# Attention and a mixture of experts on one core: one pass over all tokens per expert, with operands made ahead

## The chip, the core and the metric

The kernel runs on one core of a Trainium2 chip. The engines of a core work side by side, each with its own queue, in order: TensorE (PE in the profile, its weight loads PEld) multiplies matrices, VectorE (DVE) and ScalarE (ACT) do elementwise work and read TensorE's results from PSUM banks, GpSimd (POOL) does little here, and SyncE (SP) issues the transfers between DRAM and the on-chip memory (SBUF). The metric is the time of one execution on the device in microseconds (us), the median over runs.

## The reference

```python
scores = scale * q @ k.T + bias(relative position)      # B, H, S, D = 4, 8, 576, 64
attn = softmax(scores); x = (attn @ v), tokens 2304 x 512
P = exp(x @ w_gate - max); 8 times: rows, then columns normalised    # 2304 x 8
out = sum over e of P[:, e] * (relu(x @ w1[e]) @ w2[e])  # w1: 8 x 512 x 1024, w2: 8 x 1024 x 512
```

The inputs are float32 and are drawn at random.

## The kernel before, in words

The first 550 us or so are attention, with expert 0 of the mixture woven into its second half. The change doesn't touch that part. What follows is the mixture for experts 1 to 7, and everything here is about it.

Each float32 operand is held as two float16 parts, high and low, and a product is three matmuls (high with high, high with low, low with high). The tokens lie in four blocks of 512 and one of 256 (blocks 0 to 3, and 4). For experts 1 to 7 both layers are done with the Strassen-Winograd scheme: seven products of half-size operands in place of eight. The seven left operands of layer 1 are A11, A12, S2, S3, S1, A22, S4, made of the quarters of w1; the seven of w2 are B11, T4, B21, T2, T3, T1, B22. They sit in 14 slots (6 tiles `slot`, and 8 places in `area` where expert 0's weights were). On the token side four sums T1 to T4 per block are needed (`xt`, made by `t_prep`), beside the tokens themselves (`xa`, `xb`, `xc`).

- `l1(i)` (L1453) does layer 1 of a block: `prod1` (L1468) issues the matmuls of one product, ScalarE takes the banks out (`snap`, L1539), VectorE forms sums, and `put` (L1527 on ScalarE, L1179 or L1533 on VectorE) cuts them into high and low parts in the tiles `h`.
- `l2(i)` does layer 2 (`prod2`, L1502), with `out_` (L1591) and the addition into the accumulators `acc`, one tile of 512 columns per 128 tokens.
- `w_load` fetches the four quarters of a weight into `raw` (those of w2 lie in `xc`, over tokens), `w_max` (L1375) finds the largest magnitude on ScalarE, and `bcast_nodes` (L1205, L1210) spreads it over the partitions with two small matmuls.
- `w_make(e, w)` then makes the seven operands of a weight: sums of quarters on VectorE (L1422) and cuts into high and low (L1412 on ScalarE, L1179 on VectorE, both of 1024 columns). It writes them straight into slots, and stores a copy to DRAM (`sc_w`).

The tokens are passed over in two runs. The first takes blocks 0, 4 and 1 through experts 1 to 7, and makes the operands of the next expert at the last block of the present one, since a slot is free only when its last product is done. The second takes blocks 2 and 3 through experts 7, 1, ..., 6, and gets the operands back from DRAM (`w_fetch`). All accumulators of a run (10 tiles) stay on the chip.

The order of the instructions isn't the program's: `Plan` (a list scheduler) records each piece of work with its engine, an assumed duration, the names that it reads and writes, and a priority, and writes out each engine's queue in the order of its own assumed start times. Transfers are assumed to take 0.1 us on SP and to land 4 us later (5 us for a fetch). On the chip every queue then runs in that order, and an instruction that waits holds up those behind it. The last lines are the two runs:

```python
    runs = [
        (list(range(1, E)), [(0, pairs(0, 0)), (2, pairs(2, 4)), (1, pairs(1, 1))]),
        ([E - 1] + list(range(1, E - 1)), [(0, pairs(0, 2)), (1, pairs(1, 3))]),
    ]
...
                if last and nxt:
                    ready(nxt, 0)
                l2(i, bt, f"pcol{e}", pcols[e], n == len(experts) - 1)
                if last and nxt:
                    ready(nxt, 1)
```

## Time and profile before

| what | value |
|---|---|
| median of 3 runs | 1891.71 us (1890.39 to 1895.35) |
| the profiled execution | 1893.5 us, its span 1891.7 us |
| PE busy | 1688.3 us, 89% of the span |
| DVE busy | 1472.5 us, 78% |
| ACT busy | 1109.2 us, 59% |
| mean granted clock of TensorE | 0.952 of full speed |
| moved by DMA | 259.24 MB |

The profile comes from one execution; its span runs from the first to the last instruction, and the execution's own time is 1.8 us longer. "Busy" is the time in which an engine has an instruction in work. A granted clock of 1.00 is 2.4 GHz, 0.50 is 1.2 GHz; a number between is a mean over a stretch with both. In a time order "[4.82 <-ACT ...]" behind a row says that the engine stood for 4.82 us before it, and what released it.

### The profile page before, as it was taken

The page shows a single profiled execution, that of the slowest core. Times are in us where ns is not written, and L with a number is a line of the kernel's source. Part 1 is how long each engine was busy: PE and PEld are TensorE (multiplying, and loading weights), DVE is VectorE, ACT ScalarE, POOL GpSimd, SP SyncE. Part 2 cuts the span into 40 slices and gives each one's busy share as a digit, 9 for nine tenths or more (in the row PEclk, how much of TensorE's full clock was granted, in tenths as well). Part 3 has the DMA queues.
Part 4 walks back from the last instruction along what each step waited for, and adds up shares of the span by engine and source line. Part 5 has one row for each costly group of instructions (what it writes and reads, how often), then busy time and mean ns, then how long its engine had stood idle before and what let it go on. Part 6 is the DMA issues. An engine that isn't in the chain of part 4 may idle for free.

```text
span 1891.7 us, 39544 instructions
## 1 busy us (share of the span) xinstructions
PE 1688.3 (89%) x16286; PEld 1362.6 (72%) x16286; DVE 1472.5 (78%) x2767; ACT 1109.2 (59%) x2050; POOL 1.5 (0%) x10
## 2 busy tenths in 40 slices
PE   7676587887889599898989999898999999999998
PEld 4344354554556388787868888787888888888887
DVE  8898877877868878888887979888767666766765
ACT  7686877877866645665655646554444334434433
POOL 0000000000000000000000000000000000000000
PEclk9898699899999899998989999899999999999999
DMA  8989999999986502405042323301314314314221
GB/s 289 252 191 229 208 193 215 211 215 202 228 206 219 204 1 86 161 34 212 24 146 79 145 102 136 111 1 60 98 42 150 124 34 157 103 55 157 80 83 40
DMA packets 316149, 259.24 MB, mean 137 GB/s; under 512 B 225856, under 2 KB 269632, under 8 KB 315328
## 3 DMA queue, kind: packets, MB, share of 16 engines
q1 hardware_dynamic: 315968, 256.72, 49.2%
q8 instruction: 127, 2.08, 0.4%
q14 instruction: 54, 0.44, 0.1%
HBM read 141.19 MB, written 62.39 MB: 108 GB/s over the span
## 4 chain that ended last, share of the span: by engine, by line
PE 65%; DVE 13%; DMA 11%; ACT 6%; issue 3%; SPq 1%; DVEq 0%; ACTq 0%
PE bankA L1482 16%; PE bankA L1502 12%; PE bankB L1502 9%; PE bankE L1502 8%; PE bankE L1482 7%; DMA aT<-ah 7%; PE bankB L1482 4%; PE l L202 3%; PE pv L202 2%; PE s L202 2%; ACT area L202 2%; DVE area L202 2%; DVE ah L202 1%; DMA xc<-in_moe_w_dram 1%; DVE sb L202 1%
## 5 line engine op out<-in xcount | busy, mean ns | idle before, releaser
L1482 PEld LDWEIGHTS <-slot 128*128 128x128 f16 x5040 | 453.2, 98 | 67.8 <-issue 20.9
L1502 PEld LDWEIGHTS <-hA 128*128 128x128 f16 x2268 | 223.4, 99 | 28.9 <-DVE hA L1179 0.8
L202 PEld LDWEIGHTS <-area 128*128 128x128 f16 x2465 | 152.2, 100 | 120.3 <-issue 52.6
L1502 PEld LDWEIGHTS <-area 128*128 128x128 f16 x1512 | 150.6, 101 | 63.7 <-ACT area L1527 25.5
L1482 PE MATMUL bankE<-xt,slot 128*128 128x256 f16 (+1 forms) x1680 | 186.3, 263 | 7.8 <-ACT p L1539 6.1
L1482 PE MATMUL bankA<-xt,slot 128*128 128x256 f16 (+1 forms) x1680 | 184.9, 262 | 4.8 <-ACT u L1539 3.2
L1527 ACT ACTIVATE hA<-c 128x512 f16<-128x512 f32 x189 | 118.1, 627 | 117.8 <-DVE c L1179 117.0
L1502 PEld LDWEIGHTS <-hS 128*128 128x128 f16 x1512 | 147.5, 98 | 18.7 <-issue 1.5
L202 DVE SCALAR_TENSOR_TENSOR ah<-sb,st,ah 128x576 f16<-128x576 f32 x144 | 114.1, 814 | 37.6 <-ACT ah L202 37.0
L1585 ACT COPY u<-bankA 128x512 f32<-128x512 f32 (+1 forms) x70 | 37.9, 542 | 174.1 <-PE bankA L1502 174.0
L1179 DVE SCALAR_TENSOR_TENSOR hA<-c,hA 128x512 f16<-128x512 f32 x189 | 128.1, 686 | 13.9 <-ACT hA L1527 11.3
L202 ACT ACTIVATE ah<-sb,st 128x576 f16<-128x576 f32 x144 | 106.6, 770 | 49.7 <-DMA aT<-ah 40.4
L1502 PE MATMUL bankB<-area 128*128 128x256 f16 x756 | 101.9, 292 | 36.4 <-ACT area L1527 24.1
L202 PE MATMUL s<-qkT 128*128 128x512 f16 (+3 forms) x560 | 87.8, 310 | 51.7 <-DVE st L202 47.5
L202 ACT ACTIVATE sb<-sb,st,sms 128x576 f32<-128x576 f32 x144 | 123.5, 859 | 0.7
L202 PE MATMUL l<-area 128*128 128x512 f16 x413 | 110.2, 382 | 7.3 <-ACT ys L202 2.6
L1179 DVE SCALAR_TENSOR_TENSOR acc<-c,fs,acc 128x256 f32<-128x256 f32 x252 | 110.2, 481 | 2.2
L202 PEld LDWEIGHTS <-qkT 128*128 128x128 f16 (+1 forms) x560 | 39.2, 105 | 92.6 <-issue 68.5
L202 PE MATMUL pv<-aT,vs 128*64 128x256 f16 (+3 forms) x1176 | 80.0, 269 | 27.3 <-DMA aT<-ah 25.7
L1539 ACT ACTIVATE u<-bankA 128x512 f32<-128x512 f32 x126 | 75.0, 595 | 38.9 <-PE bankA L1482 24.6
L202 PEld LDWEIGHTS <-vs 128*64 128x64 f16 (+1 forms) x1176 | 54.4, 116 | 55.8 <-issue 49.9
L1539 ACT ACTIVATE p<-bankA 128x512 f32<-128x512 f32 x63 | 37.6, 597 | 96.2 <-PE bankA L1482 65.1
(210 smaller groups left out, 3213.9 us busy)
## 6 DMA issues: line engine op xcount, KB each, us to landing
sc_w<-area SPq DMA_DIRECT2D x48, 512.0 KB, 3.6
area<-sc_w SPq DMA_DIRECT2D x48, 512.0 KB, 4.3
bt<-sc_bias SPq DMA_DIRECT2D x32, 576.0 KB, 4.8
sc_w<-slot SPq DMA_DIRECT2D x36, 512.0 KB, 2.7
slot<-sc_w SPq DMA_DIRECT2D x36, 512.0 KB, 4.6
raw<-in_moe_w_dram SPq DMA_DIRECT2D x28, 512.0 KB, 5.1
xc<-in_moe_w_dram SPq DMA_DIRECT2D x28, 512.0 KB, 5.7
area<-const_xm_dram SPq DMA_DIRECT2D x40, 128.0 KB, 3.8
```

What stands on the lines that cost most here:

```text
L202: self.plan.record(self.name, cost, lambda: fn(*args, **kw), ins, outs, move)
L1179: vec.scalar_tensor_tensor(out=o, in0=x, scalar=s, in1=y, op0=op0, op1=op1)
L1482: pe.matmul(ps[:, jf * w : jf * w + w], t[:, a, c * 512 + f * P : c * 512 + f * P + P], x(xp, c), start=(first and jf == 0 and c == 0 and ...
L1502: pe.matmul(ps[:, j * 256 : j * 256 + 256], h[:, a, fc * w + j * P : fc * w + j * P + P], t[:, wp, fc * 256 : fc * 256 + 256], start=(firs ...
L1527: on_act(0.58, lambda: act.activation(h[:, 0, sl], x, AF.Relu if relu else AF.Copy), [r], wk)
L1539: on_act(0.55, lambda: act.activation(tmp[k], bank[b], f, scale=HS), [b], [k], 0)
L1585: on_act(0.27 * nt, lambda: act.copy(tmp[k][:, :n], bank[b][:, :n]), [b], [k], 0)
```

## The change

There is one pass. For each expert all five blocks are visited, in the order here, 0, a, 4, b, where the next expert starts with b: its token sums and accumulators are kept on the chip. For other blocks the sums `xt` (now two buffers) come from DRAM (`sc_t`), the accumulators (now 8 tiles, two sets of 4) are written to and read from `sc_y`, and one of blocks 1 to 3 at a time lies in `xc`. Blocks 1 and 2 give their places (`xb` and half of `xc`) to the raw quarters of w2. The sums of three of the five blocks are made during expert 1 rather than before it.

The operands of experts 2 to 7 are made in single steps (`w_steps`): a cut into one of two staging tiles, and at most one sum of quarters. One step is let go at each call of `paced()`, which stands after each half of a block's layer 1 and twice in layer 2; a step's ScalarE part can't be planned before the product that was last at that call (`mark`). The cut is stored to DRAM, and all 14 operands are fetched into the slots at the change of expert. The core of the diff:

```diff
-    raw.append({q: xc[:, i // 2].bitcast(F32)[:, 1024 * (i % 2) : 1024 * (i % 2) + 1024] for i, q in enumerate(BLK)})
+    raw.append(
+        {q: (xb, xc[:, 0])[i // 2].bitcast(F32)[:, 1024 * (i % 2) : 1024 * (i % 2) + 1024] for i, q in enumerate(BLK)}
+    )
     slot = [fin.tile([P, 2, 1024], F16, name=f"slot{i}") for i in range(6)]
     slot += [w1t[0][i] for i in range(4)] + [w2t[0][i] for i in range(4)]
-    XK = [["x0"], ["x1"], ["raw111", "raw112"], ["raw121", "raw122"], ["x4"]]
+    XK = [["x0"], ["raw111", "raw112"], ["raw121", "raw122"], ["x3"], ["x4"]]
     XALL = [k for l in XK for k in l]
-    acc = [fin.tile([P, DM], F32, name=f"acc{t}") for t in range(10)]
+    acc = [fin.tile([P, DM], F32, name=f"acc{t}") for t in range(8)]
...
+    mark = [0]
+    def on_unit(cost, fn, r, w):
+        mark[0] += 1
+        on_pe(cost, fn, r, [*w, f"mark{mark[0]}"])
...
-    xt = [fin.tile([P, 4, 2, 2, w], F16, name=f"xt{i}") for i, w in enumerate((256, 256, 128))]
-    sc_x = dram.tile([2, P, 2, 4096], F16, name="sc_x")
+    xt = [fin.tile([P, 4 * 2 * 2 * 256], F16, name=f"xt{i}") for i in range(2)]
+    sc_x = dram.tile([3, P, 4096], F16, name="sc_x")
+    sc_t = dram.tile([5, P, 4096], F16, name="sc_t")
     sc_w = dram.tile([E - 2, 2, 7, P, 2048], F16, name="sc_w")
+    stage = [fin.tile([P, 2, 1024], F16, name=f"stage{i}") for i in range(2)]
+    for i in range(4):
+        tmp[f"g{i}"] = stage[i // 2][:, i % 2].bitcast(F32)
...
-            i = old[USE[w][len(new)]] if old else 7 * w + len(new)
-            new[op] = i
-            t, r = slot[i], raw[w][q]
-            rk = f"raw{w}{q}"
-            on_act(1.04, lambda: act.activation(t[:, 0], r, AF.Copy, scale=s), [rk, f"scal{e}{w}"], [f"w{i}"], 2)
-            on_vec(1.27, lambda: stt(t[:, 1], r, s, t[:, 0], ALU.mult, ALU.subtract), [rk, f"scal{e}{w}"], [f"w{i}"], 2)
-            if e < E - 1:
-                k = USE[w].index(op)
-                dma(sc_w[e - 1, w, k], t.rearrange("p a n -> p (a n)"), [f"w{i}"], [f"sw{e}{w}{k}"])
+            k, r = USE[w].index(op), raw[w][q]
+            rd, at = [f"raw{w}{q}", f"scal{e}{w}"], [f"mark{mark[0]}"]
+            if e == 1:
+                t, tk, at = slot[7 * w + k], [f"w{7 * w + k}"], []
+            else:
+                j = turn[0] % 2
+                t, tk = stage[j], [f"g{2 * j}", f"g{2 * j + 1}"]
+                turn[0] += 1
+            on_act(1.04, lambda: act.activation(t[:, 0], r, AF.Copy, scale=s), rd + at, tk, 2)
+            on_vec(1.27, lambda: stt(t[:, 1], r, s, t[:, 0], ALU.mult, ALU.subtract), rd, tk, 2)
+            if e > 1:
+                dma(sc_w[e - 2, w, k], t.rearrange("p a n -> p (a n)"), tk, [f"sw{e}{w}{k}"])
...
+            plan_ = (
+                ("A11", "11"),
+                ("A22", "22", ("22", "21", "22", ALU.add)),
+                ("A12", "12", ("21", "11", "21", ALU.subtract)),
+                ("S3", "21", ("11", "22", "11", ALU.subtract)),
+                ("S2", "11", ("12", "12", "11", ALU.subtract)),
+                ("S1", "22"),
+                ("S4", "12"),
+            )
         else:
...
+        def step(op, q, *sums):
+            put(op, q)
+            for a in sums:
+                tt(*a)
+        return [lambda a=a: step(*a) for a in plan_]
...
+    seq, here = [], 3
+    for e in range(1, E):
+        a, b = (x for x in (1, 2, 3) if x != here)
+        seq += [(e, x) for x in ((here, 0, a, 4, b) if e < E - 1 else (here, 0, a, b, 4))]
+        here = b
+    visits, visit = [], []
+    for n, (e, b) in enumerate(seq):
+        if n == 0 or seq[n - 1][1] != b:
+            visits.append((e, b))
+        visit.append(len(visits) - 1)
+    todo = []
+    def paced():
+        if todo:
+            todo.pop(0)()
...
+    def t_make(b, z, ts, src):
+        x = xts(b, z)
+        t_prep(xv[src], XK[src], WID[b], [x[:, k] for k in range(4)], [[f"t{z}{k}"] for k in range(4)], ts)
+        n = 16 * WID[b]
+        dma(sc_t[b, :, :n], xt[z][:, :n], [f"t{z}{k}" for k in range(4)], [f"st{b}"])
+    def t_ready(r):
+        if r >= len(visits):
+            return
+        (e, b), z = visits[r], r % 2
+        if e == 1:
+            t_make(b, z, ("g0", "g1", "g2", "g3"), at(b))
+            return
+        m = 16 * WID[b]
+        dma(xt[z][:, :m], sc_t[b, :, :m], [f"st{b}"], [f"t{z}{k}" for k in range(4)])
+    def x_ready(n):
+        if seq[n][1] in (0, 4):
+            return
+        for _, b in seq[n + 1 :]:
+            if b not in (0, 4):
+                if b != seq[n][1]:
+                    dma(xc[:, 1], sc_x[b - 1], [f"sx{b}"], XK[3])
+                return
+    def acc_ready(r):
+        if r >= len(visits):
+            return
+        (e, b), z = visits[r], r % 2
+        if e == 1:
+            first_part(tiles_of(b, z))
+            return
+        for t, a in tiles_of(b, z):
+            dma(acc[a], sc_y[t], [f"y{t}"], [f"acc{a}0", f"acc{a}1"])
+    def acc_done(r, e):
+        b, z = visits[r][1], r % 2
+        if e < E - 1:
+            for t, a in tiles_of(b, z):
+                dma(sc_y[t], acc[a], [f"acc{a}0", f"acc{a}1"], [f"y{t}"])
...
+    w_load(2, 0)
+    w_max(2, 0)
+    acc_ready(0)
+    acc_ready(1)
+    for n, (e, b) in enumerate(seq):
+        r = visit[n]
+        i, at_end, leaves = (b, r % 2), n % 5 == 4, visit[n + 1 : n + 2] != [r]
+        nxt = e + 1 if e < E - 1 else None
+        if n % 5 == 0:
+            gate_col(e)
+            if nxt:
+                w_load(nxt, 1)
+                w_max(nxt, 1)
+                todo.extend(w_steps(nxt, 0) + w_steps(nxt, 1))
+                if nxt < E - 1:
+                    todo.insert(7, lambda e=nxt + 1: (w_load(e, 0), w_max(e, 0)))
+        l1(i)
+        x_ready(n)
+        if leaves:
+            t_ready(r + 2)
+        if at_end and nxt:
+            assert len(todo) <= 7
+            w_fetch(nxt, 0)
+        l2(i, pairs(b, r % 2), f"pcol{e}", pcols[e], e == E - 1)
+        if leaves:
+            acc_done(r, e)
+            acc_ready(r + 2)
+        if at_end and nxt:
+            assert not todo, len(todo)
+            w_fetch(nxt, 1)
```

Three places where the order of the instructions moves. The first is VectorE before the change, where layer 1 of expert 2's first block meets the end of w2's operands (`xc` holds raw quarters of w2, `area` the slots; `c`, `s` and `h` belong to layer 1, `acc` to layer 2):

```order
L1422 TENSOR_TENSOR xc_73<-xc_73 128x1024
L1533 TENSOR_TENSOR area_100<-c211_6686,area_100 128x512
L1422 TENSOR_TENSOR xc_73<-xc_73 128x1024
L1179 SCALAR_TENSOR_TENSOR area_100<-xc_73,fs15_6735,area_100 128x1024 x2
L1422 TENSOR_TENSOR xc_73<-xc_73 128x1024
L1179 SCALAR_TENSOR_TENSOR area_100<-xc_73,fs15_6735,area_100 128x1024
L1591 TENSOR_TENSOR c110_6681<-bankB0_6669,p1_6675 128x512
L1179 SCALAR_TENSOR_TENSOR area_100<-xc_73,fs15_6735,area_100 128x1024
L1179 SCALAR_TENSOR_TENSOR acc0_6697<-c110_6681,fs41_6762,acc0_6697 128x256
L1179 SCALAR_TENSOR_TENSOR acc1_6698<-c110_6681,fs41_6762,acc1_6698 128x256
L1179 SCALAR_TENSOR_TENSOR area_100<-xc_73,fs15_6735,area_100 128x1024
```

And VectorE after the change, in the middle of expert 4, whose blocks go on while expert 5's operands of w2 are made (`xb` and `xc` hold the raw quarters, `stage` the staging tiles):

```order
L1179 SCALAR_TENSOR_TENSOR c211_6686<-c211_6686,s2_6680 128x512
L1555 TENSOR_TENSOR hS3_6709<-c111_6682,hS3_6709 128x512
L1438 TENSOR_TENSOR xb_72<-xb_72 128x1024
L1555 TENSOR_TENSOR area_100<-c211_6686,area_100 128x512
L1614 TENSOR_TENSOR c110_6681<-bankB0_6669,p1_6675 128x512
L1179 SCALAR_TENSOR_TENSOR stage0_6726<-xc_73,fs27_6747,stage0_6726 128x1024
L1179 SCALAR_TENSOR_TENSOR acc0_6697<-c110_6681,fs43_6764,acc0_6697 128x256
L1179 SCALAR_TENSOR_TENSOR acc1_6698<-c110_6681,fs43_6764,acc1_6698 128x256
L1438 TENSOR_TENSOR xb_72<-xc_73,xb_72 128x1024
```

Eight operations of 1024 columns stood close together; now they stand one or two at a time between the operations of a block.

The second place is SP before the change, at a change of expert in the first pass: stores of the finished operands and loads of the next raw quarters.

```order
L1176 DMA sc_w_6727<-slot1_6692 128x2048
L1176 DMA raw21_6689<-in_moe_w1_dram 128x2x512
L1176 DMA sc_w_6727<-slot2_6693 128x2048
L1176 DMA raw22_6690<-in_moe_w1_dram 128x2x512
L1176 DMA raw11_6687<-in_moe_w1_dram 128x2x512
L1176 DMA sc_w_6727<-area_100 128x2048 x2
L1176 DMA raw12_6688<-in_moe_w1_dram 128x2x512
L1176 DMA sc_w_6727<-area_100 128x2048 x3
L1176 DMA xc_73<-in_moe_w2_dram 128x4x256
L1176 DMA sc_w_6727<-area_100 128x2048
L1176 DMA xc_73<-in_moe_w2_dram 128x4x256
```

SP after the change, at the change from the second to the third expert: the last accumulators of block 4 leave and those of another block come in, then the operands are fetched.

```order
L1176 DMA acc5_6702<-sc_y_70 128x512
L1176 DMA acc4_6701<-sc_y_70 128x512
L1176 DMA slot0_6691<-sc_w_6725 128x2048
L1176 DMA slot1_6692<-sc_w_6725 128x2048
L1176 DMA slot2_6693<-sc_w_6725 128x2048
L1176 DMA slot3_6694<-sc_w_6725 128x2048
L1176 DMA slot4_6695<-sc_w_6725 128x2048
L1176 DMA slot5_6696<-sc_w_6725 128x2048
L1176 DMA area_100<-sc_w_6725 128x2048 x3
L1176 DMA sc_w_6725<-stage1_6727 128x2048
L1176 DMA xc_73<-in_moe_w2_dram 128x4x256
L1176 DMA area_100<-sc_w_6725 128x2048 x5
```

The slots are now filled from `sc_w` at each change of expert; no store or load of the kept block's accumulators stands around the fetches. One staging store is still queued among the fetches.

The third place is SP after the change, at the change from the first to the second expert:

```order
L1176 DMA sc_w_6725<-stage0_6726 128x2048
L1176 DMA slot2_6693<-sc_w_6725 128x2048
L1176 DMA sc_w_6725<-stage1_6727 128x2048
L1176 DMA slot4_6695<-sc_w_6725 128x2048
L1176 DMA slot5_6696<-sc_w_6725 128x2048
L1176 DMA area_100<-sc_w_6725 128x2048 x2
L1176 DMA xc_73<-in_moe_w2_dram 128x4x256
L1176 DMA area_100<-sc_w_6725 128x2048
L1176 DMA sc_w_6725<-stage1_6727 128x2048
L1176 DMA xb_72<-in_moe_w2_dram 128x4x256
L1176 DMA area_100<-sc_w_6725 128x2048
```

Here three staging stores stand among the fetches.

## Rows read from the trace of the kernel before

**Rows 1.** Busy time of each engine by stretch, in us from the span's start: the start up to TensorE's first full expert, one row per expert in the first pass, one for the first expert of the second pass and one for the rest up to TensorE's end. Columns: stretch, length, busy time (instructions) of PE, PEld, DVE, ACT, POOL, granted clock, DMA share, GB/s.

```profile
630.05:744.03 113.98, 94.11 (x909) 82.99 (x908) 88.09 (x149) 67.34 (x107) 0.00 (x0) 0.91 0.20 71
744.03:848.30 104.27, 96.44 (x933) 84.88 (x931) 88.22 (x143) 61.37 (x97) 0.00 (x0) 0.97 0.31 112
...
952.70:1058.70 106.00, 97.22 (x933) 85.10 (x931) 88.28 (x143) 61.13 (x97) 0.00 (x0) 0.95 0.31 110
1058.70:1162.00 103.30, 95.99 (x933) 84.60 (x931) 88.30 (x142) 61.06 (x97) 0.00 (x0) 0.97 0.31 113
...
1370.56:1443.99 73.43, 73.43 (x674) 65.75 (x672) 49.24 (x83) 32.82 (x56) 0.00 (x0) 1.00 0.35 113
1443.99:1884.20 440.21, 440.21 (x4034) 394.42 (x4031) 295.50 (x493) 185.35 (x312) 0.00 (x0) 1.00 0.28 90
```

**Rows 2.** The order of time on TensorE: products at the start, two of the small block (24 matmuls of 128 columns), the pair of small matmuls that spreads a maximum, two successive wide products of the second pass, and the last one. Columns: start, length of the merged row, engine, line, operation, operands, shape, count.

```profile
630.05 2.88 PE L1482 MATMUL bankA<-xa,slot 128*128 128x256 f16 x24
...
666.42 0.27 PE L1205 MATMUL bankS<-ident,fs 128*1 128x128 f32 x1
...
685.92 0.38 PE L1210 MATMUL bankS<-fs,ones 1*128 1x1 f32 x2
...
694.16 1.50 PE L1482 MATMUL bankB<-xa,slot 128*128 128x128 f16 x24
695.50 1.50 PE L1482 MATMUL bankA<-xt,slot 128*128 128x128 f16 x24
...
1370.56 1.47 PE L1482 MATMUL bankA<-xa,slot 128*128 128x256 f16 x12
1371.87 1.47 PE L1482 MATMUL bankE<-xt,slot 128*128 128x256 f16 x12
...
1881.54 2.78 PE L1502 MATMUL bankB<-area 128*128 128x256 f16 x24
```

**Rows 3.** The order of time on all engines at the change from expert 1 to expert 2.

```profile
775.19 1.22 DVE L1422 TENSOR_TENSOR xc<-xc 128x1024 f32<-128x1024 f32 x1
775.39 0.60 PE L1502 MATMUL bankB<-area 128*128 128x256 f16 x2 [4.82 <-ACT area L1527]
...
778.06 2.48 DVE L1179 SCALAR_TENSOR_TENSOR area<-xc,fs,area 128x1024 f16<-128x1024 f32 x2
...
780.45 3.09 PE L1502 MATMUL bankB<-area,hA 128*128 128x256 f16 x24
```

**Rows 4.** Groups of instructions of VectorE from 675 us to the end: the cuts (L1179 on 1024 columns) and the sums (L1422) of the weights of experts 2 to 7. Columns: line, engine, operation, out<-in, shapes, count | busy us, mean ns | idle before.

```profile
L1179 DVE SCALAR_TENSOR_TENSOR area<-xc,fs,area 128x1024 f16<-128x1024 f32 x42 | 53.1, 1279 | 0.0
L1179 DVE SCALAR_TENSOR_TENSOR slot<-raw,fs,slot 128x1024 f16<-128x1024 f32 x36 | 46.0, 1279 | 0.0
...
L1422 DVE TENSOR_TENSOR xc<-xc 128x1024 f32<-128x1024 f32 x24 | 29.3, 1220 | 0.0
L1422 DVE TENSOR_TENSOR raw<-raw,raw 128x1024 f32<-128x1024 f32 x24 | 29.3, 1219 | 0.0
...
L1179 DVE SCALAR_TENSOR_TENSOR area<-raw,fs,area 128x1024 f16<-128x1024 f32 x6 | 7.7, 1281 | 0.0
```

**Rows 5.** Two stretches of 25 us, one of the first pass and one of the second, in the columns of rows 1.

```profile
825.00:850.00 25.00, 25.00 (x232) 22.40 (x230) 23.27 (x35) 17.43 (x25) 0.00 (x0) 1.00 0.14 56
...
1425.00:1450.00 25.00, 25.00 (x232) 22.41 (x229) 16.10 (x29) 8.77 (x15) 0.00 (x0) 1.00 0.66 220
```

**Rows 6.** The transfers: the first row is SP's own time for the issue of one (ns, least, median and most); in the others count, KB each and the median us from issue to landing.

```profile
L1176 SPq DMA_DIRECT2D sc_w<-slot x36: 319/320/382, 593.9 to 1170.4; - x36
...
sc_w<-area SPq DMA_DIRECT2D x48, 512.0 KB, 3.6
area<-sc_w SPq DMA_DIRECT2D x48, 512.0 KB, 4.3
...
sc_w<-slot SPq DMA_DIRECT2D x36, 512.0 KB, 2.7
slot<-sc_w SPq DMA_DIRECT2D x36, 512.0 KB, 4.6
...
acc<-sc_y SPq DMA_DIRECT2D x18, 256.0 KB, 3.0
...
sc_y<-s SPq DMA_DIRECT2D x6, 256.0 KB, 4.4
```

**Rows 7.** Who waited for whom: ScalarE for raw weights (800 to 1890 us), and SP for sums that were being stored (614 us to the end). Columns: total us, times, longest us.

```profile
ACT junk L1375 <- DMA xc<-in_moe_w_dram: 10.5, 10, 1.6
...
SPq L1176 <- DMA sc_y<-s: 7.9, 2, 5.2
```

**Rows 8.** The order of time at the start of the MoE part (token sums, L1330; the first stops of TensorE; ScalarE's wait for raw weights) and at the end (the last additions).

```profile
570.14 1.29 DVE L1330 TENSOR_TENSOR xt<-c,xt 128x512 f16<-128x512 f32 x2
...
653.89 0.37 PE L1205 MATMUL bankS<-ident,fs 128*1 128x128 f32 x1 [14.00 <-DVE fs L1384]
...
657.71 1.06 ACT L1375 ACTIVATE junk<-xc 128x1024 bf16<-128x1024 f32 x1 [1.52 <-DMA xc<-in_moe_w_dram]
...
659.39 2.72 PE L1482 MATMUL bankE<-xt,slot 128*128 128x256 f16 x12 [5.12 <-ACT p L1539]
...
1884.66 0.69 DVE L1591 TENSOR_TENSOR c<-bankB,u 128x512 f32<-128x512 f32 x1
1885.38 0.88 DVE L1179 SCALAR_TENSOR_TENSOR acc<-c,fs,acc 128x256 f32<-128x256 f32 x2
```

More of the change, by code (lines that the diff above doesn't have):

```diff
@@ L1613, in l2 @@
         out_(bb, "p1", c1, 0, 0)
+        if nt == 2:
+            paced()
         prod2(i, "S2", "T2", ba, False)
@@ L1664, in first_part @@
             )
-    def pairs(i, b):
-        if i == 2:
-            return [((16, 8), (17, 9))]
-        return [((4 * b + j, 4 * i + j), (4 * b + 2 + j, 4 * i + 2 + j)) for j in range(2)]
-    runs = [
-        (list(range(1, E)), [(0, pairs(0, 0)), (2, pairs(2, 4)), (1, pairs(1, 1))]),
-        ([E - 1] + list(range(1, E - 1)), [(0, pairs(0, 2)), (1, pairs(1, 3))]),
-    ]
-    TS = (("c110", "c220", "c210", "u4"), ("c111", "c221", "c211", "p7"))
-    def t_here(i):
-        dk = [[f"t{i}{k}"] for k in range(4)]
-        t_prep(xv[place[i]], XK[place[i]], WID[i], [xt[i][:, k] for k in range(4)], dk, TS[i % 2])
@@ new lines, in attention_sinkhorn_moe, with pairs, tiles_of @@
+    visits, visit = [], []
[7 more added lines that the diff above has]
+            todo.pop(0)()
+    def pairs(b, z):
+        if b == 4:
+            return [((16, 4 * z), (17, 4 * z + 1))]
+        return [((4 * b + j, 4 * z + j), (4 * b + 2 + j, 4 * z + 2 + j)) for j in range(2)]
+    def tiles_of(b, z):
+        return [ta for pair in pairs(b, z) for ta in pair]
```

119 lines of the change are left out of this document (37 added, 82 removed).

## The prediction, made before the result was known

> **What bounds the kernel now.** I read the stretches of the run first, one per expert, then the time order at the places where TensorE stands still, then the groups of VectorE, then the transfers.
>
> The stretches [rows 1] cut the MoE part where TensorE starts an expert's first block. In the second pass over tokens (from 1370.56 us) TensorE is busy for the whole of 73.43 us and of 440.21 us, at granted clock 1.00. There an expert's two blocks of 512 tokens take 73.43 us, so one block takes 36.7. In the first pass an expert's three blocks take 103.3 to 106.0 us, TensorE is busy for 96 to 97 of them, and the granted clock is 0.95 to 0.98. What would they take without standing still? Two blocks are 73.4. The small block has 7 products of 24 narrow matmuls, whose starts lie 1.34 us apart, and 7 of 12 wide ones at 1.31 [rows 2]: 18.55. That is 92.0 us.
>
> Now the whole. TensorE takes up the Strassen products at 630.05 and starts its last 24 matmuls at 1881.54 [rows 2]; these take 2.62, so it ends at 1884.16: 1254.1 us. Seven experts over four large blocks and one small need 7 x (4 x 36.71 + 18.55) = 1157.8. Two products (2.6) ran before 630.05, and twelve pairs of tiny matmuls that spread a weight's maximum cost 0.27 + 0.38 each [rows 2], 7.8. So 1163.0 is work and 91.1 is lost:
> - 630.05 to 744.03, the start: 114.0 less 92.0 - 2.6 + 1.3 = 90.7 leaves 23.3 lost.
> - 744.03 to 1370.56, six changes of expert: 626.5 less 6 x 92.0 and ten pairs (6.5) leaves 68.0, or 11.3 a change.
> - after that: nothing.
>
> Why is a change lost? At 775 us TensorE has stood for 4.82 us for an operand that ScalarE has only just written, and VectorE, with no gap, is in the middle of the next expert's weights (L1422, L1179 on 1024 columns); the matmuls after it run at 3.09 us per 24 where 2.62 is usual [rows 3], at a lower granted clock [rows 1]. The weights of six experts are 84 cuts and 48 sums, 165.4 us of VectorE [rows 4], 27.6 per expert. They can be written only when the old operands have been read for the last time, so all 27.6 fall between the last block's first layer and the next expert's second layer. The blocks ask VectorE for 49.24 us per two [rows 1], 24.6 each. So 24.6 + 27.6 = 52.2 us of VectorE meet about one block of TensorE, 36.7: 15.5 too much, of which 11.3 show.
>
> **The change part by part.** *Making operands at a pace.* Nothing is removed from VectorE: the same 84 cuts and 48 sums. They go to a staging tile, from there to DRAM, and are fetched into the slots at the change of expert, as the second pass does today. Per expert VectorE then has four large blocks (98.5), a small one (the first pass's 88.3 less 49.2 and 27.6, so 11.5) and the making (27.6): 137.6 of 165.4 us, 83%. Does TensorE keep going at that? Between 825 and 850 us VectorE is busy 23.27 of 25 (93%), with weights in it, and TensorE 25.00 [rows 5]. I therefore take the 68.0 as gone. Bounds: 0 to 68.0 kept.
>
> *Fetches at the change.* Fourteen of 512 KB, landing 4.6 and 4.3 us after their issue [rows 6], each released by the slot's last product and wanted one layer of a block (18.3 us) later. In the second pass the same 14 come and TensorE does not wait. New beside them: the last few staging stores and the next raw weights, some 5.7 MB in 18.3 us (seven fetches 3.7, two stores and two quarters 2.0), about 310 GB/s; the busiest stretch of the second pass has 220 GB/s at a DMA share of 0.66 [rows 5], so 310 would be a share of 0.93. Over a whole expert 28 operand transfers and 8 quarters of 0.52 MB, 14 accumulator tiles of 0.26 each way, and 5.5 MB of sums and tokens make 32 MB in 165.4 us, 190 GB/s. Cost 0; if a fetch lands 15 us late, that cover is gone.
>
> *Sums and accumulators that move.* Of 35 block visits 6 follow the same block and keep all. At the other changes accumulators go out and come in: 84 stores and 84 loads more of 256 KB, 22 more of sums, 12 more of tokens. From VectorE's last addition that is four issues (0.3 each), a landing (4.4, sc_y), four issues, a landing (3.0) [rows 6]: about 10 us. The two buffers are wanted again after one whole other visit, 18.6 us at the least. Cost by that: 0. Each change adds a wait at SP: the load stands until its store has landed, and behind it stand staging stores, raw loads and token loads. Who waits for those? A staging tile is reused two cuts later, and ScalarE, which writes it first, has TensorE's evacuations queued behind. No row shows this wait; the nearest are ScalarE's waits for raw weights, at most 1.6 us, 10.5 in 10 [rows 7]. So between 0 and 24 x 1.6 = 38 us; a gain has no way in. Most are covered, as those ten are: I take 5.
>
> The Trainium skill (DMA: Bandwidth & Descriptors, section "Two DMAs through the same engine are not ordered") says that a transfer which reads what an earlier one wrote must be held by its issuer until the earlier one has completed. The trace agrees: SP stood 7.9 us in two such waits for sc_y [rows 7]. By the rule alone SP stands 24 x 4.4 = 106 us more, out of 1160: that speaks against the change, and it is the rival "queue" below.
>
> The same page (section "Latency and other measured facts") gives 0.2 us as an average HBM access and 2 us under high load. By that a staging store would land up to 1.8 us later in the fuller traffic, and 84 of them would hold ScalarE by up to 151 us in all. The trace shows 2.7 and 3.6 us for the two kinds of store [rows 6], both among raw loads; I go by those.
>
> *The start.* Before 660 us TensorE waits 14.00 us and 5.12 us; VectorE runs without a gap through weights and token sums, then ScalarE waits for raw weights [rows 8]. The change takes three of five token-sum preparations out of here: 24 instructions of 512 columns, of which two take 1.29 (a second one adds 0.60), and 12 of half the width, taken at half of that: 18.0 us of VectorE. Bounds: 0 to 18.0 gained. The 14.00 us ended with VectorE, so a shorter list cuts them; the waits for raw weights stay. I take 13.3, so 10 of the 23.3 remain.
>
> *The first expert.* The same 18.0 us come back there: 137.6 + 18.0 = 156 of 165.4, 94%, just above the stretch that ran full. Its last staging stores also stand among its fetches. Bounds 0 to 18.0; I take 5.
>
> *The end.* The last block is the small one: the last two additions (0.69 and 0.88 us [rows 8]) at most halve: under 0.8 us, left out.
>
> Sum: 1893.5 (the profiled execution; span 1891.7) - 91.1 = 1802.4 with nothing lost, + 10 + 5 + 5 = **1822 us**. The median of the runs is 1891.71, 1.8 below the profiled one; less than I can resolve.
>
> **Rivals.**
> - *The bunch stays in part.* The last steps of each set still meet the change, because a step is released only after a marked product and its store must land before the fetch. For: in the order, stores stand among the first expert's fetches. Against: from the second expert on only one does. Half of 68.0 kept: 1822 + 34 = 1856.
> - *The start gains nothing* and the first expert pays for the moved sums: 1802.4 + 23.3 + 18.0 + 5 = 1849. For: the start also waits for the maxima of the second expert's weights, which remain. Against: VectorE's list there is 18.0 us shorter.
> - *Queue (slower than before).* Every change of block holds SP, and with it a staging store, ScalarE and TensorE. It turns the sign once a change costs more than (1893.5 - 1822) / 24 = 3.0 us; a whole landing of 4.4 beside what I took gives 1822 + 106 = 1928. For: each load does wait at SP for its store, as those two did [rows 7]. Against: SP's issues last 0.32 us [rows 6], and TensorE never waited at the second pass's fetches.
> - *The change does not do what it says.* Excluded for the kept blocks: the order shows no accumulator transfer at the expert changes.
>
> **How the numbers follow.** My forecast (1804 to 1836) 0.66; the bunch in part 0.16 and the start 0.08 (together 1836 to 1860, with tails above); queue 0.07, of which 0.05 is slower; everything hidden, below 1804, 0.03. The range 1802 to 1855 leaves out some 0.17. A change below 0.3% (5.7 us) can't be told from none: faster 0.92, same 0.03, slower 0.05.
>
> **What would show it.** Right: TensorE full across each change of expert, a period of about 165 us per expert at clock 1.00; VectorE near 83%; the idle time before the first 24-matmul product of expert 2 down to some 15 us; the DMA rate near 190 GB/s throughout. Wrong: TensorE waiting for a slot's fetch at the changes; ScalarE waiting for staging stores on sc_w; VectorE waiting for token loads in the first expert; or 30 us and more of TensorE idle between 640 and 800.

## The result, and the profile after

The changed kernel takes 1838.25 us (median of 4 runs, 1835.5 to 1842.19) against 1893.53 us before (4 runs, 1890.39 to 1895.92): a ratio of 0.9711, 95% interval 0.9686 to 0.9736. The profiled execution took 1839.06 us. The forecast was 1822 (1802 to 1855). Of the 71.5 us that it expected to go from the profiled 1893.5, 54.4 went. What it got right, and where the other 17 us stayed, is read from the stretches first. As in [rows 1] they are cut per expert: an expert's layers are 4 x 336 + 252 = 1596 matmuls, and each stretch begins with the first of the next 1596, because TensorE now begins an expert's first products before the last ones of the expert before. Columns as in [rows 1].

```profile
613.14:819.09 205.95, 185.15 (x1663) 158.14 (x1661) 174.23 (x307) 121.44 (x201) 0.00 (x0) 0.96 0.45 153
819.09:993.64 174.55, 168.89 (x1605) 150.45 (x1603) 139.72 (x228) 93.46 (x155) 0.00 (x0) 0.99 0.58 205
993.64:1161.79 168.15, 166.96 (x1605) 149.42 (x1602) 135.72 (x223) 91.52 (x150) 0.00 (x0) 1.00 0.53 190
1161.79:1328.78 166.99, 166.47 (x1605) 149.69 (x1602) 137.92 (x225) 90.32 (x148) 0.00 (x0) 1.00 0.55 193
...
1664.44:1831.61 167.17, 165.78 (x1598) 148.84 (x1595) 112.10 (x189) 69.95 (x119) 0.00 (x0) 1.00 0.25 75
```

An expert's matmuls need 4 x 36.71 + 18.55 = 165.4 us, and a stretch also holds up to two pairs of small matmuls that spread a maximum, 0.65 us each [rows 2] (the counts include instructions that reach over a border). Experts 3 to 7 together take 1831.61 - 993.64 = 838.0, of which 827 are these matmuls and 4.6 are seven such pairs: some 6 us lost in five experts. Expert 2 loses 174.55 - 165.4 - 1.3 = 8. In expert 1's stretch 64 other instructions begin, above all 48 matmuls of expert 0 at 0.22 us, together some 13.6 us; 205.95 - 165.4 - 13.6 leaves 27 lost. So 35 of the 41 us that these stretches lose lie in the first two experts.

A change of expert was where [rows 3] had TensorE standing. These 25 us, in the same columns, hold the changes from expert 2 to 3 (993.64) and from 3 to 4 (1161.79):

```profile
980.00:1005.00 25.00, 25.00 (x230) 22.23 (x228) 14.74 (x31) 7.97 (x14) 0.00 (x0) 1.00 0.52 188
1150.00:1175.00 25.00, 25.00 (x230) 22.23 (x228) 17.18 (x37) 10.16 (x18) 0.00 (x0) 1.00 0.50 169
```

TensorE is full, at granted clock 1.00, and VectorE has room (it is busy for 14.7 and 17.2 of 25 us). The making of weights still costs VectorE what it did [rows 4]: a cut takes 1279 ns, a sum 1218.

```profile
L1179 DVE SCALAR_TENSOR_TENSOR stage<-raw,fs,stage 128x1024 f16<-128x1024 f32 x35 | 44.6, 1279 | 0.5 <-ACT stage L1429 0.5
...
L1438 DVE TENSOR_TENSOR raw<-raw,raw 128x1024 f32<-128x1024 f32 x20 | 24.4, 1218 | 0.0
```

The transfers (count, KB, median us from issue to landing), beside [rows 6]:

```profile
sc_w<-stage SPq DMA_DIRECT2D x84, 512.0 KB, 3.2
acc<-sc_y SPq DMA_DIRECT2D x102, 256.0 KB, 3.8
area<-sc_w SPq DMA_DIRECT2D x48, 512.0 KB, 4.8
sc_y<-acc SPq DMA_DIRECT2D x84, 256.0 KB, 2.3
...
slot<-sc_w SPq DMA_DIRECT2D x36, 512.0 KB, 5.3
```

Fetches land 0.5 to 0.8 us later than before. Stores do not: a staging store takes 3.2, between the 2.7 and 3.6 of the two old kinds. The waits that the forecast could only bound are there now (600 to 1840 us; columns as in [rows 7]):

```profile
ACT stage L1429 <- DMA sc_w<-stage: 18.4, 10, 2.9
...
SPq L1176 <- DMA sc_y<-acc: 21.9, 25, 3.6
...
SPq L1176 <- DMA sc_w<-stage: 16.0, 7, 4.3
```

SP stood 21.9 us in 25 waits for a leaving accumulator, where the rule quoted ahead of the result gave 106 at 4.4 each: 0.9 us a wait, not a whole landing.

Now the first expert, where the loss is. The order of time on TensorE shows its two longest stops:

```profile
654.75 5.06 PE L1524 MATMUL bankB<-area,hA 128*128 128x256 f16 x23 [4.96 <-DVE area L1179]
...
783.22 0.37 PE L1504 MATMUL bankE<-xt,slot 128*128 128x256 f16 x1 [7.81 <-ACT xt L1340]
784.31 5.07 PE L1504 MATMUL bankE<-xt,slot 128*128 128x256 f16 x23 [0.71 <-DVE xt L1342]
```

The first is what is left of the start [rows 8]: 4.96 us for the last operands of w2, where before there were 14.00 and 5.12. In the first and the last row 23 matmuls take 5.06 and 5.07 us, where 24 usually take 2.62: the granted clock is 0.50 from 654.75 to 659.61 us and from 784.31 to 789.17, the lower of TensorE's two clocks. So each stop costs some 2.5 us beyond its own length. The second stop is for a token sum of expert 1's last block, block 2. What did SP and VectorE do before it? First two rows of SP, then VectorE's, each in order of time:

```profile
726.81 0.32 SPq L1176 DMA_DIRECT2D xc<-sc_x  x1
...
764.57 7.30 SPq L1176 DMA_DIRECT2D sc_w<-stage  x2
```

```profile
761.04 1.28 DVE L1179 SCALAR_TENSOR_TENSOR stage<-xb,fs,stage 128x1024 f16<-128x1024 f32 x1
...
770.20 1.28 DVE L1179 SCALAR_TENSOR_TENSOR stage<-xc,fs,stage 128x1024 f16<-128x1024 f32 x1
...
775.81 0.67 DVE L1335 TENSOR_TENSOR stage<-xc 128x512 f32<-128x512 f16 x1
...
781.23 0.69 DVE L1342 TENSOR_TENSOR xt<-stage,xt 128x512 f16<-128x512 f32 x1
```

Block 2's tokens were asked for at 726.81 and landed 4.8 us later. The sums begin at 775.81, 44 us after that, and they are formed in `stage`: the two tiles through which the paced cuts go out. Sums and steps take turns in them, and SP's 7.30 us for two stores end when the cut of 770.20 is done. On the chip the tiles themselves are seldom waited for: from 613 to 820 us a sum waits 1.7 us for a staging store, and ScalarE's cuts 2.8. VectorE comes to the sum of 775.81 without a gap, so what is late is its place in VectorE's queue, and that place the planner chose, which reckons with a tile as taken until its store has landed. The shared tiles, VectorE's amount of work, and the transfers (share 0.62 in 775 to 800 us, 0.80 in the next 25) were the three candidates for the runs.

### The profile page after: what moved, and what is told of

Same layout as the page of the kernel before. It is cut to its first block, busy times and chain, and to the rows that moved or that the text cites. A ratio compares the mean times of both kernels' runs of the same rounds, so it can differ in the third digit from the quotient of the medians.

```text
span 1837.3 us, 39912 instructions
## 1 busy us (share of the span) xinstructions
PE 1676.6 (91%) x16286; PEld 1359.5 (74%) x16286; DVE 1468.3 (80%) x2767; ACT 1103.4 (60%) x2050; POOL 1.5 (0%) x10
## 4 chain that ended last, share of the span: by engine, by line
PE 70%; DMA 12%; DVE 8%; ACT 4%; issue 2%; SPq 1%; DVEq 0%; ACTq 0%
PE bankA L1504 17%; PE bankA L1524 12%; PE bankB L1524 9%; PE bankE L1524 9%; PE bankE L1504 8%; DMA aT<-ah 6%; PE bankB L1504 4%; PE l L202 3%; PE pv L202 3%; PE s L202 2%; PE bankA L381 2%; DMA qkT<-qk 1%; DVE area L202 1%; DMA xb<-in_moe_w_dram 1%; DMA xc<-in_moe_w_dram 1%
## 5 line engine op out<-in xcount | busy, mean ns | idle before, releaser
L1179 DVE SCALAR_TENSOR_TENSOR hA<-c,hA 128x512 f16<-128x512 f32 x189 | 127.3, 685 | 11.4 <-ACT hA L1549 9.4
L1179 DVE SCALAR_TENSOR_TENSOR acc<-c,fs,acc 128x256 f32<-128x256 f32 x252 | 110.2, 480 | 1.7
L1524 PE MATMUL bankB<-area,hA 128*128 128x256 f16 x756 | 90.8, 277 | 5.0 <-DVE area L1179 5.0
L1524 PE MATMUL bankE<-area,hA 128*128 128x256 f16 x756 | 88.8, 273 | 1.5 <-ACT hA L1549 0.9
```

Source lines behind the costliest of these rows:

```text
L1179: vec.scalar_tensor_tensor(out=o, in0=x, scalar=s, in1=y, op0=op0, op1=op1)
L1524: pe.matmul(ps[:, j * 256 : j * 256 + 256], h[:, a, fc * w + j * P : fc * w + j * P + P], t[:, wp, fc * 256 : fc * 256 + 256], start=(firs ...
```

## The experiments

All are edits of the changed kernel. The kernel before ran beside each group on the same chip (medians 1895 to 1898 us there), so ratios are compared: 0.001 is 1.9 us.

The diffs here show the core of each edit; `...` stands for what is left out.

**The sums of expert 1.** Three kernels: the sums left out (the sums of the first two blocks are stored in their place), moved out of the staging tiles, and made at the start again.

```diff
 # sums_out
-        if e == 1:
-            t_make(b, z, ("g0", "g1", "g2", "g3"), at(b))
-            return
         dma(xt[z][:, :m], sc_t[b, :, :m], ...)
...
 # sums_own: formed in the places of xt[z], a fifth in junk, which the maxima (mx) write too
-                [f"mx{w}{i}"],
+                [f"mx{w}{i}", "o0"],
...
-            t_make(b, z, ("g0", "g1", "g2", "g3"), at(b))
+            t_own(b, z, at(b))
...
 # sums_start: before the weights of expert 1
+    for b in (1, 2, 4):
+        t_early(b)
...
```

> The changed kernel, with the token sums of expert 1's last three blocks not made: the sums of its first two blocks are stored to DRAM in their place and fetched (so three of five blocks compute with other blocks' sums). That takes 60 instructions, 18 us, off VectorE between 690 and 790 us. Theory 'list': VectorE's list between 565 and 830 us decides the loss of the first expert (28 us of TensorE between 613.14 and 819.09, and 7.9 in expert 2), and the 18 us are in it: 1815 to 1823 us. Rival 'queue': the loss comes from SP and the transfers at the first change (share 0.62 to 0.80 there), which this edit leaves: 1833 to 1840 us.

> The changed kernel, with the sums of expert 1's last three blocks formed in the places of the xt buffer that they end in (and one tile that was only written as waste), not in the two staging tiles; the same instructions and the same results. Theory 'list': nothing is taken off VectorE, so 1834 to 1841 us. Rival 'shared tiles': the 7.81 us stop at 783 us comes because the sums and the paced steps take turns in the same two tiles, so that block 2's sums begin 44 us after its tokens have landed: 1820 to 1828 us.

> The changed kernel, with the sums of blocks 1, 2 and 4 made at the start, as before the change (in the staging tiles, then stored), and fetched in expert 1. Theory 'list': the same 18 us stand in the same list of VectorE, only earlier, so what expert 1 gains the start pays: 1832 to 1843 us. The prediction's own steps (start 13.3 cheaper by the move, first expert 5 dearer) would give 1838 + 13 - 5 = 1846 us. Rival 'queue': the loss of the first change stays and the start pays too: 1848 to 1856 us.

| run | median us | ratio to before | interval |
|---|---|---|---|
| the change | 1838.25 | 0.9711 | 0.9686 to 0.9736 |
| sums_out | 1819.05 | 0.9594 | 0.9568 to 0.9621 |
| sums_own | 1820.69 | 0.9610 | 0.9583 to 0.9636 |
| sums_start | 1831.46 | 0.9660 | 0.9634 to 0.9687 |

The theory that I had put down first, VectorE's list, doesn't hold as the only cause: in sums_own the same instructions, in other places, save 0.0101, 19 us. The rival 'queue' (SP and the transfers, 1833 to 1840 us for sums_out) is out, since sums_out leaves them. By the total, leaving 18 us of VectorE's work out (sums_out) can't be told from sums_own (0.0016, 3 us, with an interval of 7 on either side); stretch by stretch it can. The first two experts of sums_out, and then of sums_own:

```profile
616.04:804.58 188.54, 181.67 (x1665) 156.89 (x1662) 158.86 (x277) 118.58 (x195) 0.00 (x0) 0.98 0.54 188
804.58:973.15 168.57, 166.55 (x1601) 149.22 (x1601) 135.05 (x221) 91.59 (x150) 0.00 (x0) 1.00 0.54 188
```

```profile
615.63:815.83 200.20, 185.58 (x1662) 158.42 (x1660) 170.84 (x302) 119.06 (x198) 0.00 (x0) 0.97 0.46 155
815.83:987.80 171.97, 168.66 (x1606) 150.55 (x1603) 139.42 (x227) 95.83 (x159) 0.00 (x0) 0.99 0.59 209
987.80:1154.73 166.93, 166.68 (x1604) 149.67 (x1602) 137.09 (x224) 89.99 (x149) 0.00 (x0) 1.00 0.54 193
```

In sums_own TensorE no longer waits for a sum; there the first sum of block 2 begins earlier:

```profile
768.02 0.68 DVE L1734 TENSOR_TENSOR xt<-xc 128x512 f32<-128x512 f16 x1
```

These two experts take 380.5 us in the change, 372.2 in sums_own and 357.1 in sums_out. The profiled execution of sums_own was its slowest (1828.36, 7.7 over its median), so at its median they take some 364 if the 7.7 fell there, which the record doesn't show. That puts the shared tiles at 8 to 16 us of the two experts, and the sums' own work beside the steps at 7 to 15: an estimate from single executions. The totals are alike because the later five experts differ the other way: 833 us in sums_own, 838 in sums_out and in the change, where the planner chose the order anew. Some 5 us of such a difference can be in any comparison here, and a part of the 19 us may be that.

sums_start tells of the start: with the three sums made there as before, the kernel is 0.005, 9.5 us, slower than with the sums in expert 1 and tiles of their own. The prediction's net for this move was 13.3 - 5 = 8.3. Beside sums_out, which makes them nowhere, it is 0.0066, 12.5 us, slower: what the sums cost at the start, where the prediction had 13.3. Its own number on record (1846) was wrong all the same, because it set the 5 against a first expert that pays for the tiles as well.

**The pace.** Three kernels release the 14 steps of the next expert at other times.

```diff
 # bunch_late: all at the start of the last block; none at paced()
+        while at_end and todo:
+            todo.pop(0)()
 # half_time: in the last three blocks, two per half layer
-        if todo:
-            todo.pop(0)()
+        for _ in range(2 if two[0] else 0):
+            if todo:
+                todo.pop(0)()
...
+        two[0] = n % 5 >= 2
 # release_early: all at the start of the first block; none at paced()
+        while todo:
+            todo.pop(0)()
```

> The changed kernel, with all 14 steps for the next expert released at the start of an expert's last block instead of one after each half layer. Theory 'pace': the spreading gained the 68 us; bunched, 24.6 + 27.6 us of VectorE meet 36.7 us of TensorE again, and stores and fetches come on top: at least 11.3 more per change, so 1900 to 1960 us. Rival 'one pass and copies in DRAM': the steps no longer wait for a slot's last product, and that alone gained: 1838 to 1850 us.

> The changed kernel, with the 14 steps released in an expert's last three blocks alone, two after each half layer, so that VectorE has 24.6 x 2 + 11.5 + 27.6 = 88.3 us to do beside 92 us of TensorE there (96%), as in the first pass before the change, but evenly. Theory 'room': VectorE's share in the stretch decides, and 96% leaves nothing for the order in which its results are wanted: 2 to 5 us per change, ratio 0.977 to 0.99 (1850 to 1872 us). Rival 'deadline': as long as the steps are over before the fetches, the share doesn't matter: ratio 0.968 to 0.974 (1832 to 1844 us).

> The changed kernel, with all 14 steps released at the start of an expert's first block, so that the planner may put them wherever VectorE and ScalarE have room, in place of one step per half layer. Theory 'time in hand': the steps only have to be over well before the change, and four blocks of room do that without a fixed pace: ratio 0.966 to 0.976 (1830 to 1848 us). Rival 'even pace': what counts is that VectorE is never filled for long; a bunch at an expert's start costs as one at its end does in part: at least 5 us per change, ratio 0.987 or more (1868 us).

bunch_late: 1976.95 us, ratio 1.0421 (1.0384 to 1.0458), slower than before the change and above what either theory gave. Its experts 2 and 3, and two stops in expert 3:

```profile
801.58:1000.73 199.15, 176.70 (x1604) 153.59 (x1602) 138.12 (x224) 91.30 (x149) 0.00 (x0) 0.94 0.47 161
1000.73:1194.75 194.02, 176.02 (x1604) 153.19 (x1602) 137.10 (x224) 91.93 (x149) 0.00 (x0) 0.95 0.47 166
```

```profile
1015.71 8.19 PE L1504 MATMUL bankA<-xt,slot 128*128 128x256 f16 x48 [3.24 <-DMA slot<-sc_w]
...
1053.92 2.78 PE L1524 MATMUL bankA<-area,hS 128*128 128x256 f16 x24 [3.21 <-DMA area<-sc_w]
```

Each of the experts 2 to 7 takes 24 to 32 us more than 167. TensorE now waits for fetches, 68.5 us in all after 1000 us, because an operand that is made late must still be cut, stored and fetched: without the pace the way through DRAM costs more than the old direct one (11.3 a change). So one pass with copies in DRAM gains nothing by itself; what pays is that the steps are over well before the fetches.

bunch_late also tells something of the first expert, whose sums it makes in the staging tiles as the change does, but with only 4 of the 14 cuts beside them:

```profile
613.06:801.58 188.52, 181.27 (x1660) 156.42 (x1658) 156.89 (x287) 107.17 (x183) 0.00 (x0) 0.98 0.31 108
```

It takes 188.5 us, as in sums_out, which has the steps without the sums. So neither costs TensorE anything there alone (165.4 + 13.6 and the start's 9 are 188.0). The loss comes where both stand in one queue: 200.2 us with tiles of their own, 205.95 in shared ones.

half_time: 1874.81 us, 0.9879 (0.9860 to 0.9897), where 'room' had 0.977 to 0.990. But its reason, VectorE's share, is not what the stops show: of the 24.1 us that TensorE waits for other engines between 996 and 1700 us, 21.0 end with ScalarE. In the order of time:

```profile
1124.58 1.15 ACT L1429 ACTIVATE stage<-raw,fs 128x1024 f16<-128x1024 f32 x1 [4.09 <-DMA sc_w<-stage]
...
1127.09 0.39 PE L1524 MATMUL bankA<-area,hS 128*128 128x256 f16 x2 [1.98 <-ACT hS L1549]
...
1188.66 1.06 ACT L1386 ACTIVATE junk<-xb 128x1024 bf16<-128x1024 f32 x1 [3.80 <-DMA xb<-in_moe_w_dram]
...
1190.35 2.72 PE L1504 MATMUL bankA<-xt,slot 128*128 128x256 f16 x12 [3.86 <-ACT u L1561]
```

ScalarE stands 4.09 us for a staging tile whose store has not landed, and TensorE stands behind it for hS, which ScalarE writes soon after. Between 980 and 1700 us such waits come to 26.7 us in 14 against 13.3 in 7 with the plain change (980 to 1690). This is the wait that the prediction had no row for; at the plain pace it is mostly covered, here less so. The longest stop shown, 3.86 us, stands behind another wait of ScalarE, for raw weights. half_time takes 0.0168, 32 us, more than the change; how they divide between these waits and VectorE's share was not separated.

release_early: 1854.22 us, 0.9784 (0.9769 to 0.9799), between the two theories. Its stretches say why:

```profile
614.37:836.81 222.44, 185.43 (x1666) 158.27 (x1664) 178.60 (x317) 127.39 (x208) 0.00 (x0) 0.92 0.46 159
836.81:1005.13 168.32, 166.70 (x1605) 149.76 (x1603) 136.91 (x224) 90.37 (x149) 0.00 (x0) 1.00 0.55 192
```

```profile
744.40 0.37 PE L1504 MATMUL bankE<-xt,slot 128*128 128x256 f16 x1 [21.52 <-ACT xt L1340]
```

Later experts lose 1 to 2 us each, but the first has one stop of 21.52 us for a token sum: block 1's sums stood behind the steps. Three further kernels followed that up, all on top of sums_own.

```diff
 # own_early: sums_own and release_early
 # early_steps: the maxima of the following w1 stay at their paced place
+        calls[0] += 1
+        if calls[0] == 8 and todo:
+            todo.pop(0)()
...
 # early_first: besides, the sums ahead of the steps in the planner's order
-    ... xk, wk, 2)
+    ... xk, wk, 1)
```

> The edits of sums_own and release_early together: all 14 steps released at an expert's first block, and the sums of the first expert in their own places. Theory 'time in hand': release_early lost only in the first expert (222 us there against 206), where the sums stood behind still more steps in the shared tiles, while its later experts took 168.5 us each; without the sharing the steps need no even pace: ratio 0.958 to 0.966 (within 4 us of sums_own). Rival 'even pace': the 14 us that release_early lost stay: ratio 0.968 or more.

> The edits of sums_own, with all 14 steps released at an expert's first block, but the load and the maxima of the following expert's w1 left where they were (at the eighth half layer). In own_early the 13.45 us stop at 724 us was a tiny matmul that spreads such a maximum, planned early into TensorE's queue while the maximum itself waited. Theory 'time in hand': that stop was the maxima's, not the steps', so without it the steps need no even pace: ratio 0.958 to 0.966. Rival 'even pace': experts 2 to 5 lose 5 to 10 us each in own_early without such a stop, and that stays: ratio 0.968 or more.

> The edits of early_steps, and the sums of expert 1's last three blocks planned at priority 1, ahead of the steps (2), not behind those that stand earlier in the program at the same priority. Theory 'place in the queue': the 20.46 us stop at 730 us in early_steps is TensorE waiting for sums that stand behind 14 steps in VectorE's queue; put ahead, expert 1 takes 190 to 198 us in place of 213, and the 6 us that experts 3 to 5 lose each stay: ratio 0.963 to 0.969. Rival 'work': VectorE is simply full there (16.1 of 20 us at the stop, 18.5 before it), so the steps or the sums are late whichever stands first: ratio 0.972 or more.

own_early: 1859.76 us, 0.9798 (0.9776 to 0.9819): not 'time in hand', and more than the 14 us of 'even pace'. Its longest stop was at a tiny matmul:

```profile
723.82 0.37 PE L1214 MATMUL bankS<-ident,fs 128*1 128x128 f32 x1 [13.45 <-DVE fs L1395]
```

It spreads a maximum, and the maxima and the sums share the tile `junk` in sums_own: the first sum that needs it starts on VectorE at 724.82, behind the last maximum. early_steps takes the maxima away from there: 1849.25 us, 0.9758 (0.9742 to 0.9774), again 'even pace' by the number. The stop is at the same place in the program, now at a token sum:

```profile
729.81 0.37 PE L1504 MATMUL bankE<-xt,slot 128*128 128x256 f16 x1 [20.46 <-ACT xt L1750]
```

early_first: 1844.23 us, 0.9716 (0.9700 to 0.9733), between its two theories. That stop is gone and expert 1 takes 199.40 us in place of 212.87, but expert 2 takes 175.05 in place of 167.84: half came back. So here a sum's place in the queue decided which stretch pays, and half of it was paid for in the next. In both kernels experts 3 to 5 take 170 to 173 us, where sums_own has 167 and the change 167 to 170, and early_first ends 20 us above sums_own. On top of sums_own an even pace is thus worth some 20 us beyond the deadline. It isn't shown to be worth that in general: release_early's later experts, with the same release, take 167 to 169 us, no more than the change's. Why stays open, beyond that the planner put them in another order.

**The accumulators and the kept block.**

```diff
 # no_acc: no accumulators stored or loaded at a change of block
-            dma(acc[a], sc_y[t], ...)
...
-                dma(sc_y[t], acc[a], ...)
 # no_keep: every visit is a new one
-        if n == 0 or seq[n - 1][1] != b:
+        if True:
```

> The changed kernel without the transfers of accumulators at the changes of block (84 stores and 84 loads of 256 KB left out, so the sums over experts are not kept apart by block). The prediction's own term: they cost 5 us of queue in all, so 0 to 6 us saved: ratio 0.968 to 0.9715 (1832 to 1839 us). Rival 'queue': each of 24 changes holds SP for a landing and through it staging stores and ScalarE: 15 us or more saved, ratio 0.963 or less.

> The changed kernel without the keeping: at each change of expert the block that is met twice stores its accumulators and has sums and accumulators fetched into the other buffers, like any other block (its fetch precedes its store, so additions of an expert's last block are lost). Some 24 more accumulator transfers each way and 6 more fetches of 1 MB stand near the operands' fetches. Theory 'hidden': SP and the transfers have room, 0 to 4 us dearer: ratio 0.970 to 0.9735 (1837 to 1843 us). Rival 'queue': they hold the operands' fetches back: 3 us or more per change, ratio 0.98 or more (1856 us).

no_acc: 1833.42 us, 0.9671 (0.9656 to 0.9687): 0.004 below the change, 7.6 us, with an interval of some 6 on either side. It can't be told from the 0 to 6 expected and is below the 15 at which the run's rival 'queue' began. By the profile the gain lies in the first two experts:

```profile
616.99:819.51 202.52, 183.58 (x1662) 157.24 (x1660) 172.95 (x306) 120.80 (x200) 0.00 (x0) 0.97 0.37 130
819.51:990.44 170.93, 167.20 (x1606) 149.72 (x1604) 138.41 (x227) 96.00 (x157) 0.00 (x0) 1.00 0.47 168
```

They take 373.5 us in place of 380.5, and the five after them 836.8 in place of 838.0. no_keep: 1837.08 us, 0.9695 (0.9677 to 0.9712), not to be told from the change. The keeping of a block costs and saves nothing that shows here; 24 more transfers each way are hidden.

**GpSimd.** The last edit puts the additions and subtractions of sums_own on the idle engine.

```diff
-            on_vec(0.69, lambda: vec.tensor_tensor(out=r, in0=y[0], in1=y[1], op=ALU.add), xk, wk, 2)
+            plan.add("pool", 1.1, lambda: pool.tensor_tensor(out=r, in0=y[0], in1=y[1], op=ALU.add), xk, wk, 2)
...
```

> The edits of sums_own, with the 24 additions and subtractions of the sums of expert 1's last three blocks on GpSimd, which has nothing to do there, not on VectorE: 16 x 0.69 + 8 x 0.42 = 14.4 us off VectorE. Theory 'list is long enough': with the sharing gone VectorE's list no longer decides, so within 3 us of sums_own: ratio 0.958 to 0.964. Rival 'VectorE's list': what is left of the first expert's loss falls by some 10 us: ratio 0.957 or less. The rule of the Trainium skill (SBUF, section 'Who interferes with whom') that a VectorE instruction with two SBUF inputs and a GpSimd instruction that reads SBUF shut each other out would make VectorE's own instructions beside them longer, by up to one GpSimd instruction each: ratio 0.965 or more if TensorE then waits.

own_pool: 1819.46 us, 0.9582 (0.9560 to 0.9603), not to be told from sums_own; both are faster than the change. Its first expert, in the columns of [rows 1]:

```profile
613.87:812.56 198.69, 182.40 (x1662) 155.97 (x1660) 174.94 (x279) 122.56 (x203) 37.54 (x24) 0.98 0.47 168
```

VectorE has 23 instructions less than in sums_own's first expert (279 against 302) and is busy 4 us more (174.94 against 170.84); GpSimd takes 37.54 us for its 24. So this run doesn't tell whether a shorter list would help: the list didn't get shorter.

## Why the prediction was right where it was, and where it was not

- *Making operands at a pace: right.* All of the 68.0 us was taken as gone; 8 are left in expert 2 and 6 in the five experts after it. Across the two changes shown TensorE is full, and in expert 3 VectorE's share is 135.72 of 168.15, 81%, where 83% was forecast; the transfers move 190 GB/s, as forecast. bunch_late shows that it is the steps' early release, and not the single pass or the copies, that brought this; release_early's experts 2 to 7 do as well without an even pace (1009 us together, the change's 1013). Whether paced steps in two passes would have done as well wasn't tried.
- *Fetches at the change: right.* From 820 us to the end TensorE has no wait for a fetch. bunch_late shows what it costs when that cover goes.
- *The start: right.* Ten of the 23.3 us were to remain. Between 640 and 700 us TensorE is idle for 60.00 - 53.49 = 6.5 us, and 2.5 more went to the slow matmuls after the 4.96 us stop: 9.0. The sums at the start cost 12.5 us (sums_start beside sums_out) against 13.3 forecast, and the whole move 9.5 (beside sums_own) against 8.3.
- *Sums and accumulators that move: 5 forecast, about right.* no_acc frees 7.6 us, give or take 6, and by its profile nearly all of it in the first two experts, not at every change of block; ScalarE waits 18.4 us for staging stores, of bounds 0 to 38, and most of it is covered.
- *The first expert: mis-sized, and this is where the other 17 us stayed.* The prediction took 5 from bounds of 0 to 18, by VectorE's share of 94%. Without the start's 9 the first expert lost 18, and expert 2 another 8. What was off is the company of sums and steps. A row in which TensorE ran full at 93% says nothing of sums that stand behind less urgent steps in one queue; sums alone or steps alone cost nothing (bunch_late and sums_out, 188.5 us). And the term overlooked a line of the diff: the sums of expert 1 are given the tiles g0 to g3, and these are the halves of the two staging tiles, so that the planner lets sums and steps take turns. sums_own undoes that alone and gains 19 us, 8 to 16 of them in the two experts. What is left for the sums with tiles of their own is 7 to 15 us by the stretches and 3, give or take 7, by the totals; that this part was not 5 isn't shown. sums_own comes to 1820.69 us, beside a forecast of 1822; that the two agree is partly luck, since its first two experts still lose more than was forecast and its later ones less.
- *The rivals.* The time ended between the forecast and 'the start gains nothing'. Of that rival the start's half did not occur; the other half, a first expert that pays 18 us for the moved sums, is what was measured, by a mechanism that it didn't name. 'The bunch stays in part' is excluded from expert 2 on by the full stretches, and 'queue' by SP's 21.9 us and by no_acc.

The signs named ahead of the result, in the columns of [rows 1]:

```profile
640.00:700.00 60.00, 53.49 (x465) 46.44 (x463) 53.74 (x87) 36.38 (x60) 0.00 (x0) 0.94 0.31 106
700.00:800.00 100.00, 86.45 (x839) 76.08 (x837) 84.31 (x141) 54.71 (x91) 0.00 (x0) 0.95 0.55 192
```

TensorE's idle time from 640 to 800 us is 6.5 + 13.6 = 20, below the 30 that were to count as wrong, but two thirds of it lie behind 700 us, not in the start. The period of an expert is 167 to 170 us from expert 3 to 5, where about 165 was named. ScalarE's waits for staging stores are there, and small. VectorE's waits for token loads are not; the sign that was missing from the list is TensorE waiting for a sum.

## What to carry to other kernels

Work that must be over by a deadline is worth spreading over all the time before it, and more so when its result takes a store and a fetch: the same steps cost about 1 us per expert spread out, and some 28 bunched at the end. Before two pieces of work are put on the same engine and held to be cheap by that engine's share, look which tiles they pass through: a shared scratch tile is a queue too, if only in the planner's reckoning, and here to undo it gave 19 us in all, 8 to 16 of them where the tile was shared, without an instruction less. When a waited-for result stands behind less urgent work in an in-order queue, the share of busy time doesn't show it; the row with the stop and the name of the tile does.

## What was not expected of the hardware

GpSimd was to take 14.4 us off VectorE. In the profile of own_pool an addition of 512 columns that VectorE does in 0.69 us takes GpSimd 2.4 on the average of these six:

```profile
L1734 POOL TENSOR_TENSOR xt<-xc 128x512 f32<-128x512 f16 x6 | 14.5, 2443 | 655.2 <-DMA xc<-sc_x 649.7 <-PE bankE L1524 5.6
```

and VectorE's own instructions beside it, 0.69 us elsewhere, last twice as long:

```profile
734.88 5.14 POOL L1734 TENSOR_TENSOR xt<-xc 128x512 f32<-128x512 f16 x3 [5.55 <-PE bankE L1524]
```

```profile
736.02 1.43 DVE L1555 TENSOR_TENSOR hS<-s,hS 128x512 f16<-128x512 f32 x1
737.37 1.64 DVE L1555 TENSOR_TENSOR hS<-c,hS 128x512 f16<-128x512 f32 x1
738.94 1.64 DVE L1555 TENSOR_TENSOR area<-c,area 128x512 f16<-128x512 f32 x1
```

The Trainium skill (SBUF — State Buffer, section "Who interferes with whom") says that a VectorE instruction with two SBUF inputs contends with a GpSimd instruction that reads SBUF. These three have two inputs each, and the trace agrees: moving work to the idle engine gave VectorE nothing back.
